# dV and dK summed transposed, and K^T, V^T and every dS^T turned by DMA, in an attention and gated-MLP backward kernel

## The chip, the cores and the metric

One core of one Trainium2 chip runs one program. The metric is the device time of one launch in microseconds, the median of several runs. A profile is taken from a further execution, whose own time is given beside its span.

## The reference

The kernel computes the forward result and all gradients of a block with an attention branch and a gated MLP branch, for 2048 rows of width 576, 32 heads of 128, 2048 cached keys and values a head, and a hidden width of 4608:

```python
xn = layernorm(x)
q  = (xn @ wq) per head;  p = softmax(q k^T / sqrt(128));  s = (p v, heads joined) @ wo
g  = silu((sigmoid(xn @ w_gate) * (xn @ w_up)) @ w_down)
out = x + s * g
# returned: out, and the gradients of x, k_cache, v_cache, wq, wo, w_gate, w_up, w_down
# for a given grad_out (the MLP's own input argument is constant)
```

Everything is in bf16 outside of the sums. What the change touches is the attention of one head, forward and backward together. With dO the gradient at the head's output, and delta the row sums of dO and the output:

```python
S = q k^T * scale;  P = exp(S - max);  o = P v / rowsum
dP = dO v^T;  dS = P * (dP - delta)
dV = P^T (dO / rowsum);  dK = dS^T (q * scale / rowsum);  dq = dS k
```

## The kernel before

The program has five parts in a row: the MLP forward with the layer norm, its second half, the 32 heads, the output projection with the MLP backward, and the gradients of the weights and of x. The heads take from about 490 to 3750 us of the span.

**One head.** The 2048 queries are 16 tiles of 128 rows (`qt`). A slab is one such tile by 2048 keys in bf16. In the first half of a head, for each `qt`: PE makes `sp` in two halves of 1024 keys (`s_half`, L523, two matmuls of 512 columns each), DVE scales it and keeps the running minimum of the negated scores (`sneg`, L525), ACT makes the slab `Pq` (`s_exp`, L534), and SyncE transposes the slab by DMA into `PT` (`trans_dma`, L571). In the second half, for each `qt`: PE makes `dp` (`dp_half`, L553), and DVE, with ACT's help for one of the two halves of most tiles (tile `t`, L559), makes the slab `dSq` (L556, L563), which is transposed into `dST`. Fifteen of the sixteen dS slabs are transposed by DMA; the one in `PE_DS` (number 9) is transposed by PE (`trans_pe`, L489).

`PT` feeds the products for the output o, and `dST` those for dq: `rows` and `row_mm` (L583) run 16 matmuls of 128 columns for each `qt`, four `qt` in one PSUM bank. `Pq` and `dSq` themselves feed dV and dK: `kv` and `kv_mm` (L602) take a 128x128 block of the slab as the stationary operand and 128 columns of `dOn` or `Qn` as the moving one, so that the result stands with the keys on the partitions and can be stored as it is. That is done in two passes a tensor (`half`), each of which holds two PSUM banks and runs 16 x 8 matmuls.

K^T and V^T are made on PE from the loaded tiles `Kn` and `Vn` (`prep_kt`, `prep_vt`: 16 transposes each, and two copies by DVE). So are `dOn` from dO^T and `Qn` from Q^T (`prep_don`, `prep_qn`); `proj` (L482, L483) makes Q^T and dO^T.

**What sets the order.** The heads are written out as a list of steps with positions: `at(pos, fn, ...)` for most steps, `anchor(pos, ...)` for `s_half` and `dp_half`. A head is 64 units long (`HEAD`), two units a `qt`, the first half being units 0 to 32 and the second 32 to 64; positions past 64 lie in the next head's first half. `back(x)` is position x of the head before. The list is sorted by position and issued in that order, which PE, DVE and ACT keep exactly (`MAN`). SyncE and POOL are not in `MAN`: there the scheduler orders the instructions. Each engine's queue is strictly in order.

**Buffers.** 20 slabs in all, for P and dS; `NPT` = 7 tiles for `PT` and `dST` together; two tiles with the tag `t`; one tile each of K^T, V^T, Q^T, dO^T and `Vn`, two of `Kn`. PSUM: two buffers of two banks for `sp` and `dp`, and four single banks (`ps_acc`) that the row sums, the dV and dK sums, the projections and PE's transposes share.

**Queues.** SyncE's DMA queue carries the transposes of the heads and, in the last head, five loads of `wo` (`load_wo`, L432); just after come the transposing loads `oT` of the next part (L749). POOL's DMA queue carries the loads of K, V, wq and wo and all stores.

Of the kernel before, what the change touches and what calls it, by code (L numbers as in the profile page):

```python
# [9 lines left out]
bf = mybir.dt.bfloat16  # L10
f32 = mybir.dt.float32
PSUM = bass.MemoryType.PSUM
DRAM = bass.MemoryType.DRAM
P = 128
# [81 lines left out]
def kernel(  # L96
# [6 lines left out]
    nc = tc.nc  # L103
    cfg = dict(cfg or {})
    _, S, D = A_x.shape
# [4 lines left out]
    NT = S // P  # L110
# [4 lines left out]
    CH = min(512, S)  # L115
# [30 lines left out]
    ident = pers.tile([P, P], bf, name="ident")  # L146
# [5 lines left out]
    alt = Alt(nc)  # L152
# [10 lines left out]
    with tc.tile_pool(name="pa", bufs=1) as pa:  # L163
# [159 lines left out]
        if True:  # L323
# [9 lines left out]
            with tc.tile_pool(name="a2h", bufs=1, reuse_waits="tile") as hp, \  # L333
# [12 lines left out]
                for sg in range(NT // SG):  # L346
# [7 lines left out]
                    for sl in range(SG):  # L354
# [7 lines left out]
                        for ft in range(FT):  # L362
                            for j, (n0, nn) in enumerate(ncs):
                                nc.tensor.matmul(accs[j][:, :nn], lhsT=hT_st[:, ft, :], rhs=wd_sb[:, ft, n0:n0 + nn],  # L364
                                                 start=(ft == 0), stop=(ft == FT - 1))
# [25 lines left out]
    KPC = CH // P  # L391
    NSLAB, NPT = 20, 7
    STT2 = {4, 9, 14}
    PE_P = set()
    PE_DS = {9}
    with tc.tile_pool(name="ld2", bufs=2) as ld2, tc.tile_pool(name="ld1q", bufs=1) as ld1q, \
            tc.tile_pool(name="slab", bufs=NSLAB) as slabp, \
            tc.tile_pool(name="wsneg", bufs=2) as wsneg, \
# [15 lines left out]
        def at(pos, fn, *args):  # L414
            prog.append((pos, len(prog), fn, args))
# [70 lines left out]
        def pe_transposes(src_fn, dst, g, eng):  # L486
            pt = ps_acc.tile([P, 8, P], bf, name="acct", tag="acc")
            for j in range(8):
                nc.tensor.transpose(pt[:, j, :], src_fn(g * 8 + j), ident[:])  # L489
            alt.copy(dst[:, g * 8:(g + 1) * 8, :], pt[:], eng=eng)  # L490

        def prep_kt(hs, g, eng):
            if g == 0:
                hs.KT = ld1.tile([P, S], bf, name="KT")
            pe_transposes(lambda j: hs.Kn[:, j, :], hs.KT[:].rearrange("p (t q) -> p t q", q=P), g, eng)

        def prep_vt(hs, g, eng):
            if g == 0:
                hs.VT = ld1.tile([P, S], bf, name="VT")
            pe_transposes(lambda j: hs.Vn[:, j, :], hs.VT[:].rearrange("p (t q) -> p t q", q=P), g, eng)  # L500

        def prep_don(hs, g, eng):
            if g == 0:
# [90 lines left out]
            if after:  # L594
                at(pos + step * (GQ - 1) + width + AFTER, after)

        def kv_mm(bx, hs, slabs, rhs, half, qt, j, sink):
            i, jj = j // KPC, j % KPC
            if qt == 0 and jj == 0:
                bx.acc[i] = ps_acc.tile([P, KPC, P], f32, name="acckv", tag="acc")  # L600
            k0 = (half * 2 * KPC + j) * P
            nc.tensor.matmul(bx.acc[i][:, jj, :], lhsT=slabs[qt][:, k0:k0 + P], rhs=getattr(hs, rhs)[:, qt, :],  # L602
                             start=(qt == 0 and jj == 0), stop=(qt == NT - 1 and jj == KPC - 1))
            if qt == NT - 1 and jj == KPC - 1:
                sink(bx.acc[i], i)

        def kv(pos, end, hs, slabs, rhs, half, out_dram):
            ov = out_dram.rearrange("(p t) d -> p t d", t=NT)
            bx = Box()
            bx.acc = [None, None]  # L610

            def sink(acc, i):
                c = half * 2 + i
                kv_t = stg.tile([P, KPC, P], bf, name="kv")
                alt.copy(kv_t[:], acc[:], eng=KVE[i])
                nc.gpsimd.dma_start(ov[:, c * KPC:(c + 1) * KPC, :], kv_t[:])

            n = 2 * KPC
            for qt in range(NT):
                for j in range(n):  # L620
                    at(pos + (end - pos) * (qt * n + j) / (NT * n), kv_mm, bx, hs, slabs, rhs, half, qt, j, sink)

        def o_sink(hs, g):
            gs = slice(g * GQ, (g + 1) * GQ)
# [27 lines left out]

        H1 = 2 * NT
        HEAD = 2 * H1
        XO, XQ = 12.1, 12.1
        VA, VB, KA, KB = (22, 38.0), (38.5, 53.5), (58.0, 69.5), (70.5, 82.0)
        QP, DO, KVE, PJE, OUE = (41.0, 3.0), (4.0, 2.5), "ss", "sv", "s"
        KT_AT, DON_AT, VT_AT, QN_AT = (46.3, 2, "v"), (7.2, 5, "v"), (22.2, 2, "v"), (38.3, 2, "s")
        EXP_AT, RINV_AT, PT_AT, DST_AT, AFTER = 2.1, 4.6, 2.7, 2.0, 3.5
        WO_AT = 50.0  # L660
        MAN = {mybir.EngineType.PE, mybir.EngineType.DVE, mybir.EngineType.Activation}
        for h in range(H):
            hs = Head(h)
            b = h * HEAD
            back = lambda x: b - HEAD + x if h else b - 14 + x / 8
            at(back(35.0), load_w, hs)
            at(back(35.1), load_kv, hs)
            for c in range(NCH):
                at(back(QP[0] + QP[1] * c), proj, hs, "QT", c, PJE[0])
                at(b + DO[0] + DO[1] * c, proj, hs, "dOT", c, PJE[1])  # L670
            at(b + DO[0] - 2, prep_wo, hs, "s")
            for g in range(2):
                at(back(KT_AT[0] + KT_AT[1] * g), prep_kt, hs, g, KT_AT[2])
                at(b + DON_AT[0] + DON_AT[1] * g, prep_don, hs, g, DON_AT[2])
                at(b + VT_AT[0] + VT_AT[1] * g, prep_vt, hs, g, VT_AT[2])
                at(b + QN_AT[0] + QN_AT[1] * g, prep_qn, hs, g, QN_AT[2])
            for p in range(NT // 2):
                at(b + 4 * p + 2 + RINV_AT, s_rinv, hs, p)
                at(b + max(4 * p + 2.1 + RINV_AT, DON_AT[0] + DON_AT[1] * (p // 4) + 0.5), s_scale, hs, p)
            for qt in range(NT):  # L680
                p1, p2 = b + 2 * qt, b + H1 + 2 * qt
                for hf in range(NHF):
                    anchor(p1 + hf, s_half, hs, qt, hf)
                    anchor(p2 + hf, dp_half, hs, qt, hf)
                at(p1 + EXP_AT, s_exp, hs, qt)
                if qt in PE_P:
                    for g in range(2):
                        at(p1 + 5.3 + g, trans_pe, hs.PT, hs.P, qt, "PT", g, "s")
                else:
                    at(p1 + PT_AT, trans_dma, hs.PT, hs.P, qt, "PT")  # L690
                if qt in PE_DS:
                    for g in range(2):
                        at(p2 + 4.3 + g, trans_pe, hs.dST, hs.dS, qt, "dST", g, "sv"[g])
                else:
                    at(p2 + DST_AT, trans_dma, hs.dST, hs.dS, qt, "dST")
            for g in range(NG):
                rows(b + 8 * g + XO, 2, 2, hs, hs.PT, "Vn", g, o_sink(hs, g))
                rows(b + H1 + 8 * g + XQ, 2, 2, hs, hs.dST, "Kn", g, dq_sink(hs, g))
            for half, (pv, pk_) in enumerate(((VA, KA), (VB, KB))):
                kv(b + pv[0], b + pv[1], hs, hs.P, "dOn", half, out_3[0, h])  # L700
                kv(b + pk_[0], b + pk_[1], hs, hs.dS, "Qn", half, out_2[0, h])
        bl = (H - 1) * HEAD
        assert WX + WD + 1 >= H
        for k, (h0, h1) in enumerate(((0, 8), (8, 16), (16, WX), (WX, WX + 7), (WX + 7, WX + WD))):
# [1 line left out]
                at(bl + WO_AT + 3 * k, load_wo, h0, min(h1, H - 1))  # L706
        prog.sort(key=lambda e: e[:2])
        anchors.sort(key=lambda e: e[:2])
        with tc.manual_schedule(engines=MAN):
            nxt = 0  # L710
            for (pos, _, fn, args) in prog:
                while nxt < len(anchors) and anchors[nxt][0] <= pos:
                    anchors[nxt][2](*anchors[nxt][3])
                    nxt += 1
                fn(*args)

    OB = 5
    if True:
# [208 lines left out]
        with tc.tile_pool(name="c2b", bufs=1, reuse_waits="tile") as blk, tc.tile_pool(name="c2s", bufs=2, reuse_waits="tile") as sb, \  # L927
# [25 lines left out]
            for hg in range(NHG):  # L953
                cols = slice(hg * HG * P, (hg + 1) * HG * P)
                onb, dqb = held.pop(hg)
                for hl in range(HG):
                    h = hg * HG + hl
# [124 lines left out]
```

## Time and profile before

| | us |
|---|---|
| median of 3 runs | 5135.23 |
| lowest, highest run | 5106.29, 5143.39 |
| profiled execution | 5127.52 |
| its span on the core | 5125.3 |
| PE busy | 4952.3 |
| DVE busy | 3212.2 |
| ACT busy | 2232.6 |
| POOL busy | 1368.6 |
| mean granted TensorE clock | 0.993 |

The span is the stretch from the first to the last instruction on the core. Busy times count an engine's own instructions; waiting and issuing DMA transfers do not count. PE and PEld are the matmuls and the weight loads of TensorE, which overlap. A matmul's duration in the profile includes its passage through the array, so the distance from one to the next is shorter than the duration. SPq is SyncE's sequencer: its rows are issues of DMA transfers. In the view of windows, each row gives the stretch, its length, the busy time of PE, PEld, DVE, ACT and POOL with the number of instructions, the granted clock, the DMA share (the time of all packets over that of 16 DMA engines, which can pass 1 since an engine has several packets under way) and the GB/s moved.

### The profile page before, as it was taken

The numbers are of one execution on the slowest core, as the hardware profiler recorded it, in microseconds if no ns is written. First come the engines' busy times: TensorE is split into PE (matmuls) and PEld (weight loads), VectorE is DVE, ScalarE is ACT, GpSimd is POOL, SyncE is SP. The second block draws the span as 40 slices with busy tenths as digits, with TensorE's granted clock in tenths as the row PEclk, the third lists the DMA queues.
The fourth block names the chain that finished last, engine by engine and source line by source line (L and its number), as shares of the span: only waits on it lengthen the run. The fifth ranks groups of instructions, "written<-read, shape, count | busy, mean of one in ns | idle before, by whom it ended". The sixth has DMA issues, their size and how long they took to land.

```text
span 5125.3 us, 123935 instructions
## 1 busy us (share of the span) xinstructions
PE 4952.3 (97%) x53164; PEld 3467.6 (68%) x54090; DVE 3212.2 (63%) x4928; ACT 2232.6 (44%) x2676; POOL 1368.6 (27%) x1929
## 2 busy tenths in 40 slices
PE   8989999999999999999999999999999999999999
PEld 3444777777777777777777777777755555554554
DVE  5445888888888888888888888888733222210101
ACT  3422655665566556556655665565501222100000
POOL 2122332333233323323332332233222222111000
PEclk9999999999999999999999999999999999999999
DMA  9496999999999999999999999999998776697775
GB/s 326 199 200 156 194 200 199 194 196 197 198 194 198 200 196 199 202 197 198 195 199 197 195 198 194 195 195 197 212 221 241 208 205 194 206 243 164 155 154 119
DMA packets 2729048, 1016.14 MB, mean 198 GB/s; under 512 B 2531536, under 2 KB 2659024, under 8 KB 2728496
## 3 DMA queue, kind: packets, MB, share of 16 engines
q1 hardware_dynamic: 2644384, 734.17, 82.8%
q0 software_dynamic: 84112, 273.98, 17.8%
q8 instruction: 423, 6.93, 0.5%
q14 instruction: 129, 1.06, 0.1%
HBM read 172.54 MB, written 201.00 MB: 73 GB/s over the span
## 4 chain that ended last, share of the span: by engine, by line
PE 85%; DVE 6%; DMA 5%; issue 4%; SPq 0%; ACT 0%; POOL 0%; DVEq 0%; ACTq 0%
PE acckv L602 17%; PE acc L583 15%; PE acc L1023 8%; PE dp L553 7%; PE sp L523 5%; DVE sneg L525 5%; PE accp L482 5%; PE accw L906 5%; PE accd L891 3%; PE acc L961 2%; PE acc L783 2%; PE acc L364 2%; PE dh L840 2%; PE g_ps L223 2%; PE acct L489 2%
## 5 line engine op out<-in xcount | busy, mean ns | idle before, releaser
L534 ACT ACTIVATE Pq<-sneg,nm 128x2048 bf16<-128x2048 bf16 x512 | 1024.5, 2001 | 385.4 <-DVE sneg L525 382.4
L583 PE MATMUL acc<-Kn,dST 128*128 128x128 bf16 x8192 | 1066.5, 219 | 24.2 <-DMA dST<-dSq 22.4
L602 PE MATMUL acckv<-dOn,Pq 128*128 128x128 bf16 x8192 | 1034.0, 219 | 15.1
L583 PE MATMUL acc<-Vn,PT 128*128 128x128 bf16 x8192 | 1024.9, 219 | 6.7 <-DMA PT<-Pq 4.8
L556 DVE SCALAR_TENSOR_TENSOR dSq<-dp,delta,Pq 128x1024 bf16<-128x1024 f32 x608 | 773.8, 1281 | 347.6 <-PE dp L553 246.7
L602 PE MATMUL acckv<-Qn,dSq 128*128 128x128 bf16 x8192 | 895.7, 219 | 8.4 <-issue 0.2
L602 PEld LDWEIGHTS <-Pq 128*128 128x128 bf16 x8192 | 794.5, 98 | 117.6 <-issue 0.9
L583 PEld LDWEIGHTS <-PT 128*128 128x128 bf16 x8192 | 767.3, 98 | 146.9 <-DMA PT<-Pq 6.8
L583 PEld LDWEIGHTS <-dST 128*128 128x128 bf16 x8192 | 758.9, 98 | 157.2 <-DMA dST<-dSq 28.0
L602 PEld LDWEIGHTS <-dSq 128*128 128x128 bf16 x8192 | 718.8, 98 | 99.9 <-issue 0.3
L525 DVE TENSOR_SCALAR_CACHE_REDUCE sneg<-sp,nm 128x1024 bf16<-128x1024 f32 x512 | 656.5, 1282 | 81.7 <-PE sp L523 45.4
L525 DVE TENSOR_SCALAR_CACHE_REDUCE sneg<-sp 128x1024 bf16<-128x1024 f32 x512 | 625.1, 1221 | 59.9 <-PE sp L523 42.4
L559 ACT ACTIVATE t<-dp,negdelta 128x1024 bf16<-128x1024 f32 x416 | 463.6, 1114 | 417.9 <-PE acc L583 237.3
L523 PE MATMUL sp<-KT,QT 128*128 128x512 bf16 x1764 | 548.4, 379 | 33.0 <-DVE sneg L525 26.1
L553 PE MATMUL dp<-VT,dOT 128*128 128x512 bf16 x1727 | 540.5, 379 | 0.8 <-DVE dSq L556 0.8
L542 POOL TENSOR_TENSOR dOn<-dOn,rinv_all 128x256 bf16<-128x256 bf16 x256 | 156.0, 609 | 653.0 <-DVE rinv_all L538 534.4
L563 DVE TENSOR_TENSOR dSq<-t,Pq 128x1024 bf16<-128x1024 bf16 x416 | 319.1, 767 | 0.0
L906 PE MATMUL accw<-dd_blk,xn_all 128*128 128x512 bf16 x1134 | 250.7, 379 | 1.0
L1036 DVE SCALAR_TENSOR_TENSOR junk<-dxn,xn_all 128x576 f32<-128x576 f32 x16 | 12.1, 758 | 368.8 <-ACT dxn L1031 368.8
L1023 PEld LDWEIGHTS <-cf 128*128 128x128 bf16 x2304 | 146.3, 98 | 143.1 <-DMA cf<-dg_d 4.4
L223 PEld LDWEIGHTS <-xnT 128*128 128x128 bf16 x1152 | 111.1, 99 | 161.0 <-issue 24.9
L649 POOL DMA_DIRECT2D dq_d<-dq_n x128 | 98.4, 768 | 455.4 <-DVE dq_n L648 435.9
(178 smaller groups left out, 6569.3 us busy)
## 6 DMA issues: line engine op xcount, KB each, us to landing
abh_d<-abh POOLq DMA_DIRECT2D x64, 768.0 KB, 3.8
out_dram<-kv POOLq DMA_DIRECT2D x256, 128.0 KB, 4.8
a_blk<-abh_d SPq DMA_DIRECT2D x18, 1024.0 KB, 5.9
b_blk<-abh_d SPq DMA_DIRECT2D x18, 1024.0 KB, 20.8
du_d<-dd_blk POOLq DMA_DIRECT2D x18, 1024.0 KB, 8.5
dg_d<-dd_blk POOLq DMA_DIRECT2D x18, 1024.0 KB, 11.5
h_blk<-abh_d POOLq DMA_DIRECT2D x17, 1024.0 KB, 12.4
Vn<-in_A_v_cache_dram POOLq DMA_DIRECT2D x32, 512.0 KB, 6.1
```

Source lines behind the costliest of these rows:

```text
L482: nc.tensor.matmul(acc[:], lhsT=w[:, i, :], rhs=srcT[:, i, cs], start=(i == 0), stop=False)
L523: nc.tensor.matmul(sp[:, c * CH:(c + 1) * CH], lhsT=hs.QT[:, qs], rhs=hs.KT[:, hf * HW_ + c * CH: hf * HW_ + (c + 1) * CH], start=True, st ...
L525: nc.vector.tensor_scalar(sneg[:, hf * HW_:(hf + 1) * HW_], sp[:], -SCALE, None if hf == 0 else nm[:, hf - 1:hf], op0=ALU.mult, op1=ALU.mi ...
L534: nc.scalar.activation(Pq[:], sneg[:], AF.Exp, bias=nm[:, hf:hf + 1], scale=-1.0, accum_out=hs.rs_all[:, qt:qt + 1])
L553: nc.tensor.matmul(dp[:, c * CH:(c + 1) * CH], lhsT=hs.dOT[:, qs], rhs=hs.VT[:, hf * HW_ + c * CH: hf * HW_ + (c + 1) * CH], start=True, s ...
L556: nc.vector.scalar_tensor_tensor(dSq[:, hsl], dp[:], hs.delta[:, qt:qt + 1], Pq[:, hsl], op0=ALU.subtract, op1=ALU.mult)
L559: nc.scalar.activation(t[:], dp[:], AF.Identity, bias=hs.negdelta[:, qt:qt + 1], scale=1.0)
L563: nc.vector.tensor_tensor(dSq[:, hsl], t[:], Pq[:, hsl], op=ALU.mult)
L583: nc.tensor.matmul(bx.acc[:, j, :], lhsT=T[qt][:, kt, :], rhs=getattr(hs, rhs)[:, kt, :], start=(kt == 0), stop=(kt == NT - 1))
L602: nc.tensor.matmul(bx.acc[i][:, jj, :], lhsT=slabs[qt][:, k0:k0 + P], rhs=getattr(hs, rhs)[:, qt, :], start=(qt == 0 and jj == 0), stop=(q ...
L906: nc.tensor.matmul(acc[:], lhsT=xn_all[:, st, i * P:(i + 1) * P], rhs=dd_blk[:, st, :, :], start=(st == 0), stop=(st == NT - 1))
L1023: nc.tensor.matmul(accs[sl][j][:, :nn], lhsT=ch[:, kk, sl * P:(sl + 1) * P], rhs=w_[:, n0:n0 + nn], start=(pi == 0 and kk == 0), stop=(las ...
```

## The change

All of it is in the heads.

- `prep_kt` and `prep_vt` go. `turn` makes K^T and V^T with one transposing DMA each on SyncE's queue: V^T at unit 4.62 of its head, K^T at unit 51.52 of the head before.
- `PE_DS` becomes empty: all sixteen dS slabs are transposed by DMA.
- `kv` and `kv_mm` become `kvT` and `kvT_mm`: now `dOn` or `Qn` (128 columns of one `qt`) is the stationary operand and 512 columns of the slab the moving one, so that dV and dK come out transposed. Each takes four passes (`VP`, `KP`) of 16 matmuls, one PSUM bank a pass, two passes under way at a time and a little more than that where one pair follows the other. `kv_back` turns a pair of passes back with eight transposes on PE and stores it.
- The engines of several copies change (Q^T and dO^T two each on DVE and ACT, `dOn` on ACT, `Qn` on DVE), and most positions move a little.
- SyncE joins the engines that keep the written order (`MANH`).

```diff
-    PE_DS = {9}
+    PE_DS = set()
...
-        def prep_kt(hs, g, eng):
-            if g == 0:
-                hs.KT = ld1.tile([P, S], bf, name="KT")
-            pe_transposes(lambda j: hs.Kn[:, j, :], hs.KT[:].rearrange("p (t q) -> p t q", q=P), g, eng)
-
-        def prep_vt(hs, g, eng):
-            ...
+        def turn(hs, name, src):
+            t_ = ld1.tile([P, S], bf, name=name)
+            setattr(hs, name, t_)
+            nc.sync.dma_start_transpose(t_[:].rearrange("p (t q) -> p t q", q=P), src[:].rearrange("p t d -> p (t d)"))
...
-        def kv_mm(bx, hs, slabs, rhs, half, qt, j, sink):
-            i, jj = j // KPC, j % KPC
-            if qt == 0 and jj == 0:
-                bx.acc[i] = ps_acc.tile([P, KPC, P], f32, name="acckv", tag="acc")
-            k0 = (half * 2 * KPC + j) * P
-            nc.tensor.matmul(bx.acc[i][:, jj, :], lhsT=slabs[qt][:, k0:k0 + P], rhs=getattr(hs, rhs)[:, qt, :],
-                             start=(qt == 0 and jj == 0), stop=(qt == NT - 1 and jj == KPC - 1))
-            if qt == NT - 1 and jj == KPC - 1:
-                sink(bx.acc[i], i)
-
-        def kv(pos, end, hs, slabs, rhs, half, out_dram):
+        def kvT_mm(bx, hs, slabs, rhs, c, qt, eng):
+            if qt == 0:
+                bx.acc[c] = ps_acc.tile([P, CH], f32, name="acckv", tag="acc")
+            nc.tensor.matmul(bx.acc[c][:], lhsT=getattr(hs, rhs)[:, qt, :], rhs=slabs[qt][:, c * CH:(c + 1) * CH],
+                             start=(qt == 0), stop=(qt == NT - 1))
+            if qt == NT - 1:
+                if c % 2 == 0:
+                    bx.T = wt.tile([P, 2, CH], bf, name="kvT", tag="t")
+                alt.copy(bx.T[:, c % 2, :], bx.acc[c][:], eng=eng)
+
+        def kv_back(bx, k, eng, ov):
+            pt = ps_acc.tile([P, 8, P], bf, name="acct", tag="acc")
+            for j in range(2 * KPC):
+                nc.tensor.transpose(pt[:, j, :], bx.T[:, j // KPC, j % KPC * P:(j % KPC + 1) * P], ident[:])
+            kv_t = stg.tile([P, 2 * KPC, P], bf, name="kvb", bufs=1)
+            alt.copy(kv_t[:], pt[:], eng=eng)
+            nc.gpsimd.dma_start(ov[:, k * 2 * KPC:(k + 1) * 2 * KPC, :], kv_t[:])
+
+        def kvT(spans, hs, slabs, rhs, out_dram):
             ov = out_dram.rearrange("(p t) d -> p t d", t=NT)
             bx = Box()
-            bx.acc = [None, None]
-
-            def sink(acc, i):
-                c = half * 2 + i
-                kv_t = stg.tile([P, KPC, P], bf, name="kv")
-                alt.copy(kv_t[:], acc[:], eng=KVE[i])
-                nc.gpsimd.dma_start(ov[:, c * KPC:(c + 1) * KPC, :], kv_t[:])
-
-            n = 2 * KPC
-            for qt in range(NT):
-                for j in range(n):
-                    at(pos + (end - pos) * (qt * n + j) / (NT * n), kv_mm, bx, hs, slabs, rhs, half, qt, j, sink)
+            bx.acc = [None] * len(spans)
+            for c, (pos, end) in enumerate(spans):
+                for qt in range(NT):
+                    at(pos + (end - pos) * qt / NT, kvT_mm, bx, hs, slabs, rhs, c, qt, KVE[c % 2])
+                if c % 2:
+                    at(end + KV_BACK, kv_back, bx, c // 2, KVB[c // 2], ov)
...
-        XO, XQ = 12.1, 12.1
-        VA, VB, KA, KB = (22, 38.0), (38.5, 53.5), (58.0, 69.5), (70.5, 82.0)
-        QP, DO, KVE, PJE, OUE = (41.0, 3.0), (4.0, 2.5), "ss", "sv", "s"
-        KT_AT, DON_AT, VT_AT, QN_AT = (46.3, 2, "v"), (7.2, 5, "v"), (22.2, 2, "v"), (38.3, 2, "s")
-        EXP_AT, RINV_AT, PT_AT, DST_AT, AFTER = 2.1, 4.6, 2.7, 2.0, 3.5
+        XO, XQ = 12.0, 12.1
+        VP = ((21.24, 36.99), (21.74, 37.49), (36.5, 52.05), (37.84, 53.39))
+        KP = ((52.74, 68.39), (53.91, 69.56), (68.56, 85.12), (69.89, 86.46))
+        QP, DO, KVE, PJE, OUE = (42.34, 2.11), (4.0, 2.5), "ss", ('vvss', 'vvss'), "s"
+        KT_AT, DON_AT, VT_AT, QN_AT = 51.52, (7.42, 8.02, 's'), 4.62, (38.56, 2.23, 'v')
+        EXP_AT, RINV_AT, PT_AT, DST_AT, AFTER = 2.32, 4.5, 2.72, 1.72, 3.7
         WO_AT = 50.0
+        KV_BACK, KVB = 2.62, "ss"
         MAN = {mybir.EngineType.PE, mybir.EngineType.DVE, mybir.EngineType.Activation}
+        MANH = MAN | {mybir.EngineType.SP}
...
+            at(b + VT_AT, lambda hs=hs: turn(hs, "VT", hs.Vn))
+            at(back(KT_AT), lambda hs=hs: turn(hs, "KT", hs.Kn))
...
-        with tc.manual_schedule(engines=MAN):
+        with tc.manual_schedule(engines=MANH):
```

## The prediction

> **What bounds the kernel now.** Page first, then a steady head: PE's waits, SyncE's timeline, the DMA view of one head, small windows.
>
> ```profile
> PE 4952.3 (97%) x53164; PEld 3467.6 (68%) x54090; DVE 3212.2 (63%) x4928; ACT 2232.6 (44%) x2676; POOL 1368.6 (27%) x1929
> ...
> q8 instruction: 423, 6.93, 0.5%
> ```
>
> By the page PE is the bound. PE's waits between 600 and 3700 us (31 heads) confirm it; transposes that land late cost 15.8 us in all:
>
> ```profile
> PE sp L523 <- DVE sneg L525: 20.9, 61, 0.8
> PE acc L583 <- DMA dST<-dSq: 11.0, 12, 2.6
> PE acct L489 <- DVE dq_n L648: 6.9, 31, 0.2
> PE acc L583 <- DMA PT<-Pq: 4.8, 4, 2.1
> ```
>
> A second resource stands just behind. SyncE's timeline, heads 15 and 16 (counted from 0):
>
> ```profile
> 2005.89 50.99 SPq L571 DMA_TRANSPOSE PT<-Pq  x16
> 2056.99 49.61 SPq L571 DMA_TRANSPOSE dST<-dSq  x15
> 2106.70 49.13 SPq L571 DMA_TRANSPOSE PT<-Pq  x16
> 2155.93 49.85 SPq L571 DMA_TRANSPOSE dST<-dSq  x15
> ```
>
> The rows touch: SyncE is issuing transposes all the time, 31 in a head of about 100 us. By line L571 alone one issue lasts 1.32 to 8.5 us, median near 3. It isn't data that they wait for. The seventh dS slab of the last row's head is finished by this DVE row at 2172.42; its transpose, seventh in order, is issued four microseconds later:
>
> ```profile
> 2171.74 0.68 DVE L563 TENSOR_TENSOR dSq<-t,Pq 128x1024 bf16<-128x1024 bf16 x1
> 2176.51 3.40 SPq L571 DMA_TRANSPOSE dST<-dSq  x1
> ```
>
> So the transposing queue is nearly full as well. What fills it, from the DMA view of 2005.8 to 2106.6 us and from short windows (the last two numbers are DMA share and GB/s):
>
> ```profile
> q1 hardware_dynamic: 63736, 16.07, 101.7%
> q0 software_dynamic: 1184, 3.44, 12.1%
> q8 instruction: 10, 0.16, 0.6%
> ```
>
> ```profile
> 2158.80:2160.20 1.40, 1.35 (x23) 1.16 (x21) 0.54 (x1) 1.31 (x2) 1.38 (x4) 1.00 1.46 15
> 2160.40:2161.40 1.00, 1.00 (x16) 0.76 (x13) 1.00 (x2) 0.00 (x0) 1.00 (x1) 1.00 1.27 289
> 2166.00:2168.40 2.40, 2.35 (x28) 1.69 (x27) 1.64 (x2) 1.29 (x3) 0.48 (x1) 1.00 1.14 210
> 2178.80:2180.20 1.40, 1.40 (x9) 0.60 (x7) 1.40 (x3) 0.00 (x0) 0.00 (x0) 1.00 0.37 6
> 2180.40:2182.00 1.60, 1.60 (x27) 1.36 (x24) 0.89 (x2) 0.57 (x1) 1.34 (x2) 1.00 1.28 287
> ```
>
> Undisturbed, transposes move about 208 GB/s, so one of 0.524 MB takes 2.52 us. Every ten microseconds they nearly stop for 1.4 us (15 and 6 GB/s), then run at 288 for about 1.6 us, which regains (288 - 208) / 208 x 1.6 = 0.6 us: a stop costs 0.8. I put these stops down to instruction fetches: a head has ten (q8), and 6.93 MB over the 108182 PE rows of the program's listing is 64 bytes a row, so q8 is PE's program. The plain copies of the software queue take 12.1% of 100.8 us, 12.2 us.
>
> Queue per head: 31 x 2.52 + 10 x 0.8 + 12.2 = 98.3 us. The period is (3622.20 - 596.15) / 30 = 100.87 us, from the first PT issues of heads 1 and 31, so 2.6 us are left over for waits and restarts.
>
> **The change part by part.** PE: single matmuls in its timeline stand 0.216 us apart at 512 columns and 0.0555 at 128.
>
> - dV and dK: 512 narrow matmuls (28.4 us) become 128 wide ones (27.6 us).
> - Transposes that leave: 16 for K, 16 for V, 16 for dS tile 9, 48 x 0.0555 = 2.7 us. Those that turn dV and dK back: 32, 1.8 us.
> - PE per head: from 168 x 0.216 + 1109 x 0.0555 = 97.8 us to 296 x 0.216 + 581 x 0.0555 = 96.2 us.
>
> DVE loses the K^T and V^T copies and half of tile 9's (4 x 0.69 + 0.68 = 3.4 us), and swaps two dO copies for two Q copies of the same shape. ACT gains four copies of 128x1024 at 1.0 us and loses one, +3.0; dOn's copies and Qn's change places; its eight casts stay. DVE is busy 84 and ACT 60 of 100 us, so all this lies beside PE. POOL issues four stores of twice the size for eight, the same bytes, and gains 2.2 us.
>
> SyncE's queue: from 31 to 34 transposes of one shape. V^T goes behind PT 0 and ahead of fifteen PT; K^T of the next head behind dST 8 and ahead of seven dST, and tile 9 is added there. Their sources were loaded tens of microseconds earlier, so they hold the queue for their service only. No row shows K^T or V^T; bounds from rows of the same shape are 0.524 MB at 288 GB/s, 1.8 us, and 49.85 / 15 = 3.3 us. I take 2.52, the undisturbed rate. Written order by itself changes nothing in steady heads, since PT and dST follow each other as before: nothing.
>
> Fetches: the listing has 82582 PE rows after, 25600 fewer, 800 of a head's 2554. Ten fetches become 6.9.
>
> Queue per head after: 34 x 2.52 + 6.9 x 0.8 + 12.2 = 85.7 + 5.5 + 12.2 = 103.4 us, plus what remains of the 2.6. With seven tiles for PT and dST and PE waiting, the next slabs are always ready, so I keep 1.0: **104.4 us against 100.87**. The 1.6 us that PE saves vanish in waits of acc on PT and dST.
>
> What the queue hides: three dV/dK sums now hold PSUM banks for short stretches where two did, and kvT keeps one of the two t buffers until it is turned back, so that ACT's next t waits for DVE's product (at most 0.7 us each, some five a head, with the kvT casts behind it on ACT). Without the 8 us by which the queue exceeds PE these could cost 0 to 3.5 us.
>
> Ends: the first K^T by DMA needs 4.2 us or more to land, where 16 transposes and two copies took some 2.5: +2. After the last head PE waited 9.4 us for one dST that an oT transpose had overtaken on SyncE; written order mends that, but puts the five wo loads (4.3 MB) among the last dST, and the turn-back adds about 3. Together I take +4 for both ends, bounds -6 and +14.
>
> Sum: 3.5 x 31 + 4 = 113 us. The profiled execution took 5127.5 us (span 5125.3), 0.15% under the median of 5135.23. **Forecast: 5240 us.** With 0 to 2.6 us left over it is 5211 to 5290.
>
> **Rivals.**
>
> A, the queue gives way and PE stays the bound (this is the faster side). It decides if a transpose costs under (98 - 12.2 - 5.5) / 34 = 2.36 us, only 6% less than I take; 288 GB/s after each stop shows that the engines can do 1.8. Against it: with slabs ready and waiting, steady stretches ran at 203 to 210, and sixteen PT took 49 to 51 us. PE then needs 96.2 us plus some 1.8 of waits, 98.0: 2.9 x 31 = 90 less, 5042 us with the ends. The Trainium skill (Advanced Engine Details and Errata, X-Bar Transpose (TRN2)) expects 350 to 400 GB/s of such transposes, as fast as regular DMAs. By that, an estimate, 34 would need some 50 us and this rival would hold; the windows here show 210, and 288 at best, so the trace disagrees.
>
> B, the fetch stops cost their full 1.4 us. Then a transpose takes (98.3 - 14 - 12.2) / 31 = 2.33 us and the queue after 34 x 2.33 + 9.7 + 12.2 = 101.1, with 1.0 left over 102.1: +38 and the ends, 5170 us, within 1%. For it: the stops are that long. Against: the faster stretches after them.
>
> C, no relief: the fetches matter nothing, and every transpose costs what the queue gives on average now, 98.3 / 31 = 3.17 us. 34 x 3.17 + 1.0 = 108.8: +246 and the ends, 5377 us. For it: 49.85 us for fifteen dST; against it: the stops stand at the fetches.
>
> D, the change doing nothing is out: the listing shows every edit.
>
> **How the numbers follow.** Forecast 0.5, A 0.2, B 0.17, C 0.13. The measurement tells about 1%, 51 us, from no change. Faster: A, 0.2. Within 1%, to 5187: B and a little of the forecast's lower side, 0.2. Slower: 0.6. The range leaves out the lower half of A and the upper half of C: 5045 to 5350; the forecast's own is 5211 to 5290.
>
> **What would show it.** Right: SyncE's rows touch in every half; q8 falls to about 323 packets; PE's waits are led by acc on PT and dST, hundreds of microseconds, and the waits on sneg vanish; PE busy near 92% in the heads; period 103 to 106 us. Wrong: a period under 100 us with gaps between SyncE's rows (A), or stretches above 225 GB/s without a stop before them.

## The result, and the profile after

The changed kernel takes 5317.14 us in the median of four runs, the kernel before 5131.08 us on the same chip: 1.0361 times as long, 95% interval 1.0331 to 1.0392. The profiled execution took 5315.42 us, with a span of 5313.5 us and a mean granted clock of 0.981.

The page of the changed kernel: busy time of the engines, the queue q8 (number, packets, MB, share), and the chain that ended last by engine.

```profile
PE 4966.2 (93%) x40520; PEld 2933.0 (55%) x41290; DVE 3108.2 (58%) x4768; ACT 2312.2 (44%) x2772; POOL 1302.2 (25%) x1801
...
q8 instruction: 323, 5.29, 0.4%
...
PE 71%; DMA 19%; DVE 4%; ACT 3%; issue 2%; SPq 1%; POOL 0%; DVEq 0%; ACTq 0%
```

PE's share of the span fell from 97% to 93%, and DMA's share of the chain rose from 5% (before) to 19%. The stretch from 600 to 3700 us in the view of windows, first before, then after the change:

```profile
600.00:3700.00 3100.00, 3013.59 (x38495) 2412.30 (x39167) 2594.43 (x3779) 1829.60 (x2026) 1002.40 (x1405) 1.00 1.15 198
600.00:3700.00 3100.00, 2870.77 (x25002) 1800.19 (x25494) 2363.37 (x3432) 1805.76 (x2009) 888.66 (x1219) 0.98 1.13 201
```

The DMA engines move as much as before, 198 and 201 GB/s, while PE is busy for less of the time. What PE waits for between 600 and 3700 us, the changed kernel (us in total, times, longest):

```profile
PE acc L578 <- DMA PT<-Pq: 96.5, 92, 4.2
PE acc L578 <- DMA dST<-dSq: 87.5, 38, 3.9
PE acct L489 <- ACT kvb L40: 9.7, 29, 0.3
PE dp L548 <- DVE dSq L551: 7.2, 27, 0.3
```

The transposed slabs now cost PE 184 us of waits where they cost 15.8 before, and the waits on `sneg` are gone. The bank that waits for the turn-back's copy (`kvb`) costs 0.3 us a head, and `KT` and `VT` do not occur at all: they are never late themselves. SyncE's timeline of the changed kernel, one head and a little more:

```profile
2037.21 29.44 SPq L566 DMA_TRANSPOSE dST<-dSq  x9
2066.70 2.26 SPq L495 DMA_TRANSPOSE KT<-Kn  x1
2069.35 21.53 SPq L566 DMA_TRANSPOSE dST<-dSq  x7
2091.05 3.74 SPq L566 DMA_TRANSPOSE PT<-Pq  x1
2094.84 2.97 SPq L495 DMA_TRANSPOSE VT<-Vn  x1
2097.92 47.83 SPq L566 DMA_TRANSPOSE PT<-Pq  x15
```

The rows still touch: SyncE issues transposes all the time, 34 in a head, and between 600 and 3600 us no pause from one issue to the next is longer than half a microsecond. The period, from the first use of `wo_h` on PE in heads 1 and 31 (588.1 and 3789.4 us), is 106.71 us, where it was 100.87.

Of the 188.2 us that the span grew by, 175.2 came between those two points (30 heads of 5.84 us), 12.5 between the last head and the next part, and 3.6 after it; up to head 1 the change gained 3.1.

### The profile page after: what moved, and what is told of

Read it like the earlier page. It is cut to its first block, busy times and chain, and to the rows that moved or that the text cites. A ratio compares the mean times of both kernels' runs of the same rounds, so it can differ in the third digit from the quotient of the medians.

```text
span 5313.5 us, 98320 instructions
## 1 busy us (share of the span) xinstructions
PE 4966.2 (93%) x40520; PEld 2933.0 (55%) x41290; DVE 3108.2 (58%) x4768; ACT 2312.2 (44%) x2772; POOL 1302.2 (25%) x1801
## 3 DMA queue, kind: packets, MB, share of 16 engines
q14 instruction: 128, 1.05, 0.1%
## 4 chain that ended last, share of the span: by engine, by line
PE 71%; DMA 19%; DVE 4%; ACT 3%; issue 2%; SPq 1%; POOL 0%; DVEq 0%; ACTq 0%
PE acc L578 12%; DMA PT<-Pq 10%; PE acckv L595 10%; PE acc L1022 7%; PE dp L548 6%; DMA dST<-dSq 6%; PE accw L905 4%; PE sp L518 4%; PE accp L482 4%; DVE sneg L520 3%; PE accd L890 3%; PE acc L782 2%; PE acc L960 2%; PE acc L364 2%; PE dh L839 2%
## 5 line engine op out<-in xcount | busy, mean ns | idle before, releaser
L578 PE MATMUL acc<-Kn,dST 128*128 128x128 bf16 x8192 | 982.8, 224 | 122.2 <-DMA dST<-dSq 110.2
L578 PE MATMUL acc<-Vn,PT 128*128 128x128 bf16 x8192 | 968.9, 220 | 117.5 <-DMA PT<-Pq 105.0
L578 PEld LDWEIGHTS <-dST 128*128 128x128 bf16 x8192 | 696.3, 100 | 550.9 <-DMA dST<-dSq 135.3
L578 PEld LDWEIGHTS <-PT 128*128 128x128 bf16 x8192 | 680.8, 98 | 551.1 <-DMA PT<-Pq 170.6
L595 PE MATMUL acckv<-Pq,dOn 128*128 128x512 bf16 x1888 | 711.8, 381 | 2.0 <-POOL dOn L537 1.3
L595 PE MATMUL acckv<-dSq,Qn 128*128 128x512 bf16 x1857 | 695.4, 393 | 1.7
L548 PE MATMUL dp<-VT,dOT 128*128 128x512 bf16 x1952 | 602.0, 387 | 8.0 <-DVE dSq L551 8.0
L595 PEld LDWEIGHTS <-Qn 128*128 128x128 bf16 x2048 | 204.5, 101 | 55.1 <-issue 14.0
L595 PEld LDWEIGHTS <-dOn 128*128 128x128 bf16 x2048 | 199.1, 98 | 56.3 <-POOL dOn L537 8.8
L40 ACT CAST kvT<-acckv 128x512 bf16<-128x512 f32 x256 | 145.4, 583 | 127.7 <-PE acckv L595 126.2
```

The costliest lines, as they stand in the source:

```text
L548: nc.tensor.matmul(dp[:, c * CH:(c + 1) * CH], lhsT=hs.dOT[:, qs], rhs=hs.VT[:, hf * HW_ + c * CH: hf * HW_ + (c + 1) * CH], start=True, s ...
L578: nc.tensor.matmul(bx.acc[:, j, :], lhsT=T[qt][:, kt, :], rhs=getattr(hs, rhs)[:, kt, :], start=(kt == 0), stop=(kt == NT - 1))
L595: nc.tensor.matmul(bx.acc[c][:], lhsT=getattr(hs, rhs)[:, qt, :], rhs=slabs[qt][:, c * CH:(c + 1) * CH], start=(qt == 0), stop=(qt == NT - 1))
```

## The experiments

Periods are all taken as above, each from one profile. All ratios are to the kernel before on the same chip.

| kernel | transposes a head | q8 packets (PE's program) | period, us | median, us | ratio, 95% interval |
|---|---|---|---|---|---|
| before | 31 | 423 | 100.87 | 5131.08 | |
| changed | 34 | 323 | 106.71 | 5317.14 | 1.0361 [1.0331, 1.0392] |
| 1 dV, dK transposed alone | 31 | 335 | 101.40 | 5153.73 | 1.0038 [1.0024, 1.0052] |
| 2 longer program for PE | 34 | 419 | 108.06 | 5355.48 | 1.0436 [1.0406, 1.0467] |
| 3 K^T, V^T back on PE | 32 | 331 | 101.93 | 5179.37 | 1.0093 [1.0063, 1.0123] |
| 4 dS 9 back on PE | 33 | 327 | 105.36 | 5270.45 | 1.0260 [1.0227, 1.0293] |
| 5 dV, dK stored twice | 34 | 323 | 109.69 | 5422.36 | 1.0547 [1.0504, 1.0590] |
| 6 SyncE in the scheduler's order | 34 | 323 | 107.59 | 5358.41 | 1.0431 [1.0387, 1.0475] |
| 7 `wo` loaded early | 34 | 323 | 106.78 | 5331.20 | 1.0377 [1.0334, 1.0420] |
| 8 before, plus three transposes | 34 | 411 | 108.25 | 5366.79 | 1.0437 [1.0398, 1.0475] |
| 9 before, with the copies' engines | 31 | 423 | 102.87 | 5206.91 | 1.0141 [1.0116, 1.0165] |
| 10 before, in written SyncE order | 31 | 423 | 100.97 | 5139.31 | 1.0002 [0.9984, 1.0020] |
| 11 K^T, V^T made once | 32 | 323 | 101.51 | 5165.00 | 1.0058 [1.0037, 1.0080] |
| 12 as 11, without dS 9 | 31 | 323 | 99.62 | 5096.91 | 0.9909 [0.9873, 0.9944] |

The theory is the forecast's: the transposing queue sets the period, and three more transposes cost more in it than the shorter program for PE gives back. Its rivals: PE's new order stalls of itself; the written order or the `wo` loads do it; the plain copies or the fetches do.

### The number of transposes alone

The cleanest runs keep the changed kernel and only leave transposes out; PE's program and the order stay. They leave out part of the work, so that only their times are of use. The first makes K^T and V^T in head 0 and uses them in every head:

```diff
+        once = {}
...
         def turn(hs, name, src):
-            t_ = ld1.tile([P, S], bf, name=name)
+            if name in once:
+                setattr(hs, name, once[name])
+                return
+            t_ = once[name] = ld1.tile([P, S], bf, name=name)
```

> The changed kernel with K^T and V^T made by transposing DMA in head 0 only and used by every head: left out are the other heads' K^T and V^T. The queue has 32 transposes a head for 34, with the same program for PE (q8 323 packets) and the same SyncE order otherwise. Theory Q (the transposing queue sets the period, at some 2.65 us a transpose as the two kernels' periods together give it): the period falls from 106.7 by 5.3 to 101.4 us and the time to 5317 - 165 = about 5150 us, with acc on PT and dST still leading PE's waits. By my own 2.52 us: 101.7 and 5160, which this run does not tell from it. Rival S (PE's new order stalls of itself and the queue only fills the time): the period stays near 106 and the time above 5280. Rival F (K^T and V^T are cheap, the cost is elsewhere on SyncE): 104 to 106 us, 5230 to 5300.

The second leaves out the transpose of dS tile 9 too and uses that of tile 8 in its place:

```diff
+                elif qt == 9:
+                    at(p2 + DST_AT, lambda hs=hs: hs.dST.__setitem__(9, hs.dST[8]))
                 else:
                     at(p2 + DST_AT, trans_dma, hs.dST, hs.dS, qt, "dST")
```

> As the run with 32 transposes (the other heads' K^T and V^T left out), and dS tile 9 is not transposed either: the transposed tile 8 is used in its place too, so that part of dq is left out. 31 transposes a head, as many as before, with the changed kernel's PE work (96.2 us) and 323 packets on q8. Theory Q: 31 x 2.65 + 6.9 x 0.45 + 12.3 = 97.6 and the 1 to 3 us left over, 98.5 to 100.5 us a head; PE with some 1.8 of waits for banks needs 98.0. So about 99.3 and 5317 - 7.4 x 31 = 5088 us, under the kernel before. Rival S: above 5280. If dS 9 is nearly free, as its move to PE alone suggested (1.35 us with 1.8 us of PE work added), the period stays within 1.5 us of the run with 32: 5100 to 5150.

Measured: 101.51 and 99.62 us a head, 5165 and 5097 us. Two transposes less are 5.20 us less, **2.60 us each**; the third gives 1.89. Each period comes from one profile; by the medians, over the 31 heads that lack them, a transpose is 2.5 us, give or take 0.3. Waits of PE between 600 and 3600 us, first with 32 transposes:

```profile
PE acc L582 <- DMA PT<-Pq: 66.6, 76, 2.7
PE acc L582 <- DMA dST<-dSq: 23.0, 28, 3.0
```

then with 31, and the same stretch of that kernel in the view of windows:

```profile
PE acc L582 <- DMA PT<-Pq: 37.3, 45, 2.7
PE acc L582 <- DMA dST<-dSq: 11.5, 11, 5.0
```

```profile
600.00:3600.00 3000.00, 2931.64 (x26414) 1845.35 (x26413) 2439.85 (x3557) 1867.73 (x2081) 917.22 (x1256) 1.00 1.13 199
```

With 31 transposes PE is busy 97.7% of the stretch and the waits on transposes are down to 48.8 us: PE is nearly the bound, and that may be why the third transpose saved less than the other two. That PE's new order stalls of itself is refuted: the same order with three transposes fewer is 0.9% faster than the kernel before. This is no gain that a whole kernel has, since nothing does the work of the transposes left out; experiment 1, which does it on PE, is below.

### The transposes added to the kernel before

Experiment 8 puts the three added transposes and the written SyncE order into the kernel before, and keeps its narrow dV and dK:

```diff
-    PE_DS = {9}
+    PE_DS = set()
...
+            at(b + 4.62, lambda hs=hs: turn(hs, "VT", hs.Vn))
+            at(back(51.52), lambda hs=hs: turn(hs, "KT", hs.Kn))
...
-                at(back(KT_AT[0] + KT_AT[1] * g), prep_kt, hs, g, KT_AT[2])
...
-                at(b + VT_AT[0] + VT_AT[1] * g, prep_vt, hs, g, VT_AT[2])
...
-        with tc.manual_schedule(engines=MAN):
+        with tc.manual_schedule(engines=MAN | {mybir.EngineType.SP}):
```

> The kernel before with K^T, V^T and all sixteen dS tiles by DMA in written order, but dV and dK as before in 128-column matmuls: 34 transposes and 9.6 fetches a head, the same as the run with the cut matmuls. Theory Q: the same time as that run, 5355 us, within 20, which says that making dV and dK transposed is worth some 38 us by its shorter program and nothing else. Rival P (the changed order of PE's steps costs time by itself): well under 5317.

5366.79 us, period 108.25, and PE's waits between 600 and 3700 us:

```profile
PE acc L588 <- DMA dST<-dSq: 143.9, 89, 3.9
PE acc L588 <- DMA PT<-Pq: 91.8, 100, 2.6
```

So the three transposes alone add 7.38 us a head to the kernel before, 2.46 each, and the rest of the change, the transposed dV and dK above all, takes 1.54 of it back. It does so with 88 packets fewer on q8 (411 to 323), 2.75 a head: 0.56 us each, if that is all.

Experiment 1 is the other half, transposed dV and dK alone, with K^T, V^T and dS tile 9 back on PE:

```diff
-    PE_DS = set()
+    PE_DS = {9}
...
-            at(b + VT_AT, lambda hs=hs: turn(hs, "VT", hs.Vn))
-            at(back(KT_AT), lambda hs=hs: turn(hs, "KT", hs.Kn))
+            for g in range(2):
+                at(back((57.5, 61.5)[g]), prep_kt, hs, g, "v")
+                at(b + (27.0, 30.0)[g], prep_vt, hs, g, "v")
```

> Only the transposed dV and dK of the change are kept (with its positions); K^T, V^T and dS tile 9 are turned on PE again: 31 DMA transposes a head instead of 34. Theory Q (SyncE's transposing queue sets the period of a head, each transpose worth about 2.7 us): the queue needs 106.7 - 3 x 2.7 = 98.6 us, PE 96.2 + 2.7 = 98.9 us plus some waits; period 99.5 to 101, time 5080 to 5130 us, level with the kernel before or a little under it. Rival P (the new order of PE's steps, three PSUM banks for the sums and one t buffer less are what stalls PE, and the late transposes are only where it shows): PE has more to do than after the change, so 5317 us or more.

```profile
PE acct L489 <- ACT kvb L40: 29.9, 61, 0.7
PE acc L588 <- DVE VT L42: 13.6, 31, 0.7
PE acc L588 <- POOL dOn L547: 4.1, 10, 0.7
...
PE acc L588 <- DMA PT<-Pq: 1.3, 2, 1.0
```

5153.73 us, above the expected 5080 to 5130. The waits on transposes are all but gone: PE is the bound, with 98.8 us of work a head (the forecast's 96.2 and the 48 transposes that came back make 98.9) and other waits of some 1.6 us. Of these 1.0 are waits for the bank of `kvb`, among those that the prediction put at 0 to 3.5 us, laid bare; those behind the copy of `VT` come with the transposes put back. This run computes everything with 31 transposes by DMA, and it is 0.4% slower than the kernel before.

### Which of the added transposes

Experiment 3 takes only K^T and V^T back to PE (the second half of the diff above), experiment 4 only dS tile 9 (its first half).

> The changed kernel with K^T and V^T on PE again, all sixteen dS tiles by DMA: 32 transposes a head. Theory Q: two transposes less, 106.7 - 5.4 = 101.3 us a head, about 5145 us. Rival P: PE has 1.8 us more a head, 5317 to 5375 us.

> The changed kernel with dS tile 9 turned on PE again, K^T and V^T by DMA: 33 transposes a head. Theory Q: one transpose less, 104.0 us a head, about 5231 us. Rival P: PE has 0.9 us more a head, 5317 to 5345 us.

Experiment 3, PE's waits between 600 and 3700 us:

```profile
PE acct L489 <- ACT kvb L40: 30.1, 60, 0.9
PE acc L588 <- DMA PT<-Pq: 26.5, 38, 1.7
PE acc L588 <- DVE VT L42: 12.3, 31, 0.6
PE acc L588 <- DMA dST<-dSq: 12.1, 16, 1.6
```

K^T and V^T account for 4.78 of the 5.84 us: with them back on PE only 38.6 us of waits on transposes are left, and the rest is PE's own. Both runs came out 34 to 39 us above what was expected. Tile 9 saved only 1.35 us a head where a transpose is 2.60, and PE kept waiting:

```profile
PE acc L578 <- DMA PT<-Pq: 138.4, 116, 6.2
PE acc L578 <- DMA dST<-dSq: 25.2, 33, 1.5
```

PE is not the bound there, so its added work does not explain that. In the view of windows the DMA engines moved 198 GB/s in this kernel between 600 and 3700 us, and 201 in the changed one: the queue had one transpose less to carry, but carried less in the same time. Why this one transpose gave half of its price stays open.

### The fetches

Experiment 2 cuts each wide matmul of dV and dK in four with the same stationary operand, 768 PE rows a head more, and changes no other work:

```diff
-            nc.tensor.matmul(bx.acc[c][:], lhsT=getattr(hs, rhs)[:, qt, :], rhs=slabs[qt][:, c * CH:(c + 1) * CH],
-                             start=(qt == 0), stop=(qt == NT - 1))
+            for j in range(KPC):
+                nc.tensor.matmul(bx.acc[c][:, j * P:(j + 1) * P], lhsT=getattr(hs, rhs)[:, qt, :],
+                                 rhs=slabs[qt][:, c * CH + j * P:c * CH + (j + 1) * P],
+                                 start=(qt == 0 and j == 0), stop=(qt == NT - 1 and j == KPC - 1))
```

> The changed kernel with each 512-column matmul of dV and dK cut into four of 128 columns (same products, same 34 transposes): 768 more PE instructions a head, so by the size of PE's program three more instruction fetches, and PE time 0.8 us more, which lies under the queue. Theory Q with the fetch price of the prediction (0.8 us a fetch): +2.4 us a head, +77 us, 5394 us. Theory Q without a price for fetches: 5317 us, within 10. Rival P (PE bound by its order): +0.8 us a head, 5340 us.

```profile
q8 instruction: 419, 6.86, 0.5%
```

96 packets more, three a head; the period grows from 106.71 to 108.06: **0.45 us for a fetch**. The time of 5355 us lies between the two values expected, 5394 with the full price and 5317 with none. By the medians the two kernels differ by 38 us, and the intervals of their ratios leave 16 to 61, so the price lies between 0.2 and 0.6 us: the fetches do cost something, but less than the 0.8 that the windows of the kernel before gave.

A rival here is PE's own added work, which could be up to 0.8 of the 1.35 us. Against it: PE waits longer for transposed slabs, 209 us where it was 184. And in experiment 8 PE has 1.1 us less to do than in the changed kernel (97.8 - 2.7 = 95.1 against 96.2 us) and 2.75 fetches more, and is slower all the same.

### The plain copies

Experiment 5 stores dV and dK a second time, to scratch memory, 1.05 MB a head on POOL's queue:

```diff
+        extra = []
...
             nc.gpsimd.dma_start(ov[:, k * 2 * KPC:(k + 1) * 2 * KPC, :], kv_t[:])
+            n2 = len(extra)
+            x_d = dram.tile([P, 2 * KPC, P], bf, name=f"kvx{n2}_d")
+            extra.append(x_d)
+            nc.gpsimd.dma_start(x_d[:, :, :], kv_t[:])
```

> The changed kernel with every store of dV and dK made twice, the second time to a scratch buffer: 1.05 MB a head more on POOL's software queue (3.44 MB took 12.3 us of all 16 DMA engines, so 3.7 us more), nothing more on SyncE's queue or PE. Theory Q as the prediction has it (plain copies stop the transposes, microsecond for microsecond): +3.7 us a head, +118 us, about 5435 us. Rival S (the limit is SyncE's own issuing of a transpose, and copies beside it cost nothing): within 15 us of 5317.

The period grew by 2.98 us: what the software queue moves is taken from the transposes, 2.8 us for a MB. That supports the sum in which copies and transposes are added, but at four fifths of its price: by 12.2 us for 3.44 MB it would have been 3.7 us.

### The order

Experiment 6 lets the scheduler order SyncE again (`MAN` for `MANH`); it puts K^T ahead of the last two PT and V^T ahead of the last dST. Experiment 7 loads `wo` at unit 14 of the last head instead of 50.

> The changed kernel with SyncE's order left to the scheduler again, as in the kernel before; its listing puts K^T ahead of the last two PT and V^T ahead of the last dST, both earlier than the written order does. Prediction: the order is worth nothing in steady heads, the queue being busy all the time; the end of the last head may move by 10 us either way: 5317, within 20. Rival (the written order is what stalls): 5200 us or less.

> The changed kernel with the five loads of wo in the last head moved from units 50 to 62 to units 14 to 26. In the profile after, PE waits 6.0 and 6.3 us for two dST that such loads had pushed back. Theory: 12 us less, 5305 us, if the PT they now push back are not waited for as long; 5317 if they are.

Written order did no harm: without it the median is higher, 41 us above the 5317 that was expected, though the intervals of the two ratios touch. Its profile has PE's waits moved from dST to PT:

```profile
PE acc L578 <- DMA PT<-Pq: 178.3, 134, 3.8
PE acc L578 <- DMA dST<-dSq: 41.6, 50, 4.5
```

Early `wo` loads gained nothing either: from the first use of `wo_h` in the last head to that in the next part it took 151.4 us, where the changed kernel took 149.7 and the kernel before 137.2.

### Parts of the change on the kernel before

Experiment 9 gives the kernel before the changed engines for the copies of Q^T, dO^T, `dOn` and `Qn`, written SyncE order and early `wo` loads; experiment 10 gives it the last two alone.

```diff
-        QP, DO, KVE, PJE, OUE = (41.0, 3.0), (4.0, 2.5), "ss", "sv", "s"
-        KT_AT, DON_AT, VT_AT, QN_AT = (46.3, 2, "v"), (7.2, 5, "v"), (22.2, 2, "v"), (38.3, 2, "s")
+        QP, DO, KVE, PJE, OUE = (41.0, 3.0), (4.0, 2.5), "ss", ("vvss", "vvss"), "s"
+        KT_AT, DON_AT, VT_AT, QN_AT = (46.3, 2, "v"), (7.2, 5, "s"), (22.2, 2, "v"), (38.3, 2, "v")
-        WO_AT = 50.0
+        WO_AT = 14.0
...
-        with tc.manual_schedule(engines=MAN):
+        with tc.manual_schedule(engines=MAN | {mybir.EngineType.SP}):
```

> The kernel before, all its matmuls and its 31 transposes a head, with three small things taken from the change: the copies' engines (dOn on ACT, Qn on DVE, two Q and two dO copies on each), SyncE in written order, and the wo loads of the last head earlier (units 14 to 26). Theory: PE stays the bound at 97.8 us a head with the queue just under it; its waits on sneg (20.9 us in 31 heads) go, and so do the 9.4 us for the overtaken last dST: 25 to 30 us less than before, 5105 us. If the queue rather than PE sets the pace of the kernel before: within 10 us of it.

> The kernel before with SyncE in written order and the wo loads of the last head at units 14 to 26, copies as they were. Theory: only the 9.4 us for the overtaken last dST go: 5125 us, 0.2% under before.

Both missed. Experiment 10 made no difference; experiment 9 was 1.4% slower, by a wait that was not foreseen (600 to 3700 us):

```profile
PE accp L482 <- DVE Qn L42: 69.9, 30, 2.3
PE sp L523 <- DVE sneg L525: 21.1, 62, 0.7
```

`Qn`'s copy stands behind DVE's other work and holds a PSUM bank for which the projections wait, 2.3 us a head; the `sneg` waits, which were to vanish, stayed. In the changed kernel the same copy on DVE shows no such wait. No run beats the kernel before and computes all of it; experiment 10 equals it.

## Why the prediction was right, and where it was off

The forecast was 5240 us, slower by a queue that overfills. The direction, the mechanism and its signs hold, but the time lies 77 us above it, beyond the forecast's own 5211 to 5290 and within the range.

- **The bound moves from PE to SyncE's queue.** Shown: leaving transposes out of the changed kernel brings the time back and below the kernel before (experiments 11, 12), adding them to the kernel before makes it slower by 4.4% (experiment 8). The rows touch, q8 fell to 323 as computed, PE was busy 2870.77 of 3100 us (92.6%) between 600 and 3700, and the `sneg` waits went. The period of 106.71 lies just above the 103 to 106 that were given.
- **Price of a transpose, 2.52 us.** Nearly right: 2.60 in the full queue. Three cost 7.8 us instead of 7.6. Rival A needed less than 2.36 and PE as the bound; the price by the medians alone would not exclude it, but the period of 106.71 us and the touching rows do. A transpose in 2.60 us is 0.524 MB / 2.60 us = 202 GB/s. The 350 to 400 GB/s that the Trainium skill (Advanced Engine Details and Errata, X-Bar Transpose (TRN2)) expects of transposes were not reached in this queue.
- **A fetch gives back 0.8 us: mis-sized.** Experiment 2 gives 0.45, so 3.1 fetches gave back 1.4 us and not 2.5: 1.1 us a head. That the stops are fetches holds: in the trace a q8 packet starts at 2158.64 and at 2178.49 us, just ahead of the two stops that the forecast shows. The fast stretch behind a stop was cut short. Over all fetches of that kernel between 600 and 3600 us without a plain copy close by (102), the queue moved more than its usual 197 GB/s from 2 to 4 us after the packet's start, not for 1.6 us, and fell behind by 0.6 us in all; in the changed kernel it was 0.75 (40 fetches). Rival B took the same stop at 1.4 and is out; C, for which a fetch costs nothing, has its 3.17 us a transpose against it too.
- **"I keep 1.0" of the 2.6 left over: mis-sized.** Of the 5.84 us, 7.8 - 1.4 = 6.4 are explained, so what was left over shrank by about 0.6 and not by 1.6: 1.0 us a head. That it would go once the slabs were ready was an argument, without a row. In one thing it was right: SyncE's pauses of more than half a microsecond between two transposes, 1.65 us a head before (600 to 3600 us), are gone. But a transpose lands some 6 us after its issue, so others are under way in such a pause, and the time did not fall by as much. The small gaps stay: about 0.1 us after each of 34. What else makes up the rest was not isolated.
- **The two together,** 2.1 of the 2.3 us a head by which the forecast was short, are most of the 75 us between the 188 by which the span grew and the 113 of the forecast's sum; the rest lies at the ends.
- **PE's 1.6 us vanish in waits.** Right: with 34 transposes nothing of them shows in the time. With 31 they do, in the 0.9% of experiment 12, where no one does the work of the other three.
- **The copies, the banks, `kvT` hidden by the queue.** Right: 0.3 us a head for `kvb` in the changed kernel, 1.0 in experiment 1, where the queue covers nothing.
- **The ends, +4.** They came to 13 us, just inside the bounds of -6 and +14. The first K^T cost nothing (the start gained 3.1 us, where +2 was charged). The last head did: 12.5 us. PE's timeline of the changed kernel there:

```profile
3890.33 0.61 PE L578 MATMUL acc<-Kn,dST 128*128 128x128 bf16 x4 [6.01 <-DMA dST<-dSq]
...
3910.06 0.71 PE L578 MATMUL acc<-Kn,dST 128*128 128x128 bf16 x5 [6.30 <-DMA dST<-dSq]
```

  Two waits of 6 us on dST, and one of 4.7 us on `oT`, replace the one of 9.4. In the changed kernel no `oT` is issued ahead of a dST any more, as forecast, and the five `wo` loads stand among the last dST. Written order alone does not mend it: in experiment 10 an `oT` still goes ahead of the last dST, and PE waits 11.8 us for that one. SyncE's timeline there:

```profile
3735.97 7.51 SPq L749 DMA_TRANSPOSE oT<-on_d  x1
3743.59 6.26 SPq L571 DMA_TRANSPOSE dST<-dSq  x1
```

  With the `wo` loads early (experiment 7) the waits on the dST before the last are 2.4 us at most, which puts the two waits of 6 us down to the loads; but there an `oT` goes ahead of the last dST again, for which PE waits 6.8 us, and the waits on PT grow. From one kernel's profile to the next this stretch varies from 136 to 151 us, so how much of the 12.5 belongs to the change stays open.

## What to carry to other kernels

Before work is moved from a busy engine to a queue, add up the queue as closely as the engine: here PE was 97% busy and looked like the only bound, but by the forecast's sum the transposing queue was 97% full, and three more transposes of 2.6 us, less what the fetches gave back, cost 5.8 us a head where PE was to gain 1.6. Nor do the new dV and dK pay without the added transposes: with K^T, V^T and tile 9 back on PE the kernel is 0.4% slower than before, and only with that work left out altogether is it 0.9% faster. Slack that a sum cannot name ("left over") should be kept whole in the forecast until a row shows what ends it.

## What was not expected of the hardware

- A fetch of PE's program stops the transposes for 1.4 us in the windows, but is worth 0.45 us (experiment 2) to 0.56 (experiment 8) of the period; the queue regains more than half of it in the faster stretch behind.
- Plain stores take their time from the transposes: 1.05 MB more a head, 2.98 us more.
- The granted clock is lower where PE waits longest: 0.981 in the changed kernel, 0.977 in experiment 5, 0.992 in experiment 12, 0.993 before. The trace shows how. In nearly every head of the changed kernel PE stands still for 2 to 4 us, most often waiting for dST late in the second half, and runs at half the clock behind that, here in PE's timeline and in the view of windows:

```profile
2077.10 0.46 PE L578 MATMUL acc<-Kn,dST 128*128 128x128 bf16 x4 [3.13 <-DMA dST<-dSq]
```

```profile
2077.30:2080.70 3.40, 3.40 (x19) 1.90 (x17) 0.97 (x1) 0.00 (x0) 0.00 (x0) 0.50 1.13 220
2081.00:2085.00 4.00, 3.95 (x40) 2.59 (x39) 3.63 (x7) 1.27 (x3) 0.55 (x1) 1.00 1.16 214
```

  Between the two points of the period the changed kernel has 31 such stretches of 3.4 or 6.8 us, and each begins 2 to 5 us after PE came to a stop; the kernel before has one, experiment 12 two. So PE is slowed too, to 2778.29 / 3000 x 106.71 = 98.8 us busy a head where experiment 12 takes 2931.64 / 3000 x 99.62 = 97.4, but behind the late transposes: the wait comes first, and in the stretch shown the DMA engines go on at 220 GB/s while PE is slow.
